# A copy on GpSimd ahead of each pair of row scatters, reading a tile of the Fourier step before

## The chip, the cores and the metric

One core of a Trainium2 chip runs the whole program. The metric is the device time of one execution in microseconds; the time before is the median of three executions. A profile was taken of one more execution.

## What is computed

Three parts follow one another. The Fourier part takes `x` (8 batches of 3072 rows of 256 numbers) through an FFT over the rows and one over the columns and keeps the real part. Each of the 24,576 rows that result is a token. A token whose score is not positive goes on unchanged; every other one is given to one of eight experts (argmax of eight logits), whose two matrices with a relu between them add to the row. At the end every row goes through a 256 to 2048 to 256 network with a rational activation.

```python
X = np.fft.fft(np.fft.fft(x, axis=1), axis=2).real        # 8 x 3072 x 256
do = X @ w_skip > 0;  e = argmax(X[do] @ w_gate)
X[do] += gate * (relu(X[do] @ w1[e]) @ w2[e])
h = X @ w_in
g = (a0 + a1*h + a2*h*h + a3*h**3) / (1 + |b0|*|h| + |b1|*h*h + 1e-6)
out = g @ w_out
```

## The kernel before

All matrix products run in pairs of 16-bit numbers (a high and a low half), so most tiles come twice, as `h` and `l`.

**Fourier part.** One loop (lines 609 to 641) makes 98 steps, `n` from 0 to 97; a batch takes 12 of them. In step `n`, in this order of issue:

- `s1_hi` (line 235, ScalarE) copies out the first-stage result of the chunk before;
- `s2` (lines 250 to 266): 12 matmuls with the first-stage tiles (line 260), then ScalarE writes the high half `o2h` (line 264) and VectorE the low half `o2l` (line 265). These tiles come from a pool of three buffers;
- `s3` for the tiles of two steps earlier (lines 308 to 310 on TensorE, `ev` on ScalarE at 314, three VectorE instructions at 315 to 317 that write finished rows and logits);
- `s1_lo` (lines 245 and 246);
- in two steps of three, as long as there is input (up to `n` = 83), the next first-stage chunk: loads of `x`, a split into halves (lines 192, 194 on ScalarE, 204 on VectorE; for three chunks of eight GpSimd makes the low half, line 202) and 24 matmuls (lines 225 to 227);
- one step of every open `route_steps` generator, and one of the generators that convert the weights (lines 386 to 433) and the coefficients (574).

`route_steps` (line 319) works on a finished batch. Seven of its steps find expert, gate and slot of every row with small VectorE instructions; the last of them writes the slot numbers `si` (line 358). Then come 24 row scatters (line 361): each is an indirect DMA, issued by GpSimd, that sends 128 rows of 258 numbers from SBUF to their slots in the DRAM table `xs`. In the loop `per` is 2: a pair of scatters is issued in each of 12 steps of the loop. For batch `bb` these are the steps from 12 bb + 20 on. What is written step by step is only the order on GpSimd's own queue, in which there is nothing but scatters, the low halves of line 202 and one memset; a scatter waits for its `si`, for its rows and for the scatter eight before it, and for nothing else of the step. The rows live in ten buffers (parts of the tiles `mw` and `third`); one is written again two steps after its second pair was issued (line 315 waits for those transfers). What remains of batch 6 when the loop ends (6 of its 12 pairs) is issued right behind the loop, and batch 7 is scattered in threes during the first tiles of the last part.

**Last part.** From line 1155 on, 48 tiles of 512 rows go through the rational network, with the expert work woven in. It takes most of the time. GpSimd runs the subtraction of line 1006 and the output scatters of line 1029 there. The first tile needs rows of batches 0 to 5 in `xs`, a conversion (line 885), a transpose by DMA (line 888) and the matmuls of line 897.

Of the kernel before, what the change touches and what calls it, by code (L numbers as in the profile page):

```python
# [8 lines left out]
F32 = mybir.dt.float32  # L9
F16 = mybir.dt.float16  # L10
# [7 lines left out]
B, SEQ, D = 8, 3072, 256  # L18
# [111 lines left out]
def program(tc, x, w_skip, w_gate, w1, w2, w_in, w_out, a, b, f1, cs, tw, tok, ut, small, lt8, slot, out):  # L130
    nc = tc.nc
    pe, act, dve, pool, sp = nc.tensor, nc.scalar, nc.vector, nc.gpsimd, nc.sync
    es = ExitStack()
    with es:
# [22 lines left out]
        cst = fa.enter_context(tc.tile_pool(name="cst", bufs=1))  # L157
# [16 lines left out]
        def new_u():  # L174
            return ps.tile([128, 2, 512], F32, tag="u", name="u")
# [56 lines left out]
        def s1_hi():  # L232
            if s1_open:
                u, oh, _, _ = s1_open[0]
                act.activation(oh, u[:, :, 0:384].rearrange("p h (q c) -> p h c q", q=4), AF.Copy)

        def s1_lo():

            if s1_open:
                u, oh, ol, c = s1_open.pop(0)  # L240
                if c < 7:
                    dve.tensor_tensor(out=ol, in0=u[:, :, 0:384].rearrange("p h (q c) -> p h c q", q=4), in1=oh, op=ALU.subtract)
                    return
                for h in range(2):
                    pe.matmul(u[:, h, 0:384].rearrange("p (q c) -> p c q", q=4), lhsT=nid[:], rhs=oh[:, h], start=False, stop=True, skip_group_check=True)  # L245
                act.activation(ol, u[:, :, 0:384].rearrange("p h (q c) -> p h c q", q=4), AF.Copy)

        o2 = {}

        def s2(bb, gp):  # L250
            u = ps.tile([128, 2, 512], F32, tag="u", name="u")
            for s in range(2):
                g = 2 * gp + s
                o = u[:, s, 0:CB]
                n = 0
                for h in range(2):
                    lh = o1[bb, "h"][:, h].rearrange("p c q -> p (c q)")[:, g * 128:g * 128 + 128]
                    ll = o1[bb, "l"][:, h].rearrange("p c q -> p (c q)")[:, g * 128:g * 128 + 128]
                    for st, mv in ((lh, 0), (lh, 1), (ll, 0)):
                        pe.matmul(o, lhsT=st, rhs=f2t[:, h, mv, :], start=(n == 0), stop=(n == 5))  # L260
                        n += 1
            th = o2p.tile([128, 2, CB], F16, tag="o2h", name="o2h")
            tl = o2p.tile([128, 2, CB], F16, tag="o2l", name="o2l")
            act.activation(th[:], u[:, :, 0:CB], AF.Copy, scale=2.0 ** -8)
            dve.scalar_tensor_tensor(out=tl[:], in0=u[:, :, 0:CB], scalar=2.0 ** -8, in1=th[:], op0=ALU.mult, op1=ALU.subtract)
            o2[bb, gp] = (th, tl)

        rows = {}
        lgs = {}
# [49 lines left out]
        def route_steps(bb, new_u, per=2):  # L319
            lg = lgs.pop(bb)  # L320
            rws = [rows.pop((bb, i)) for i in range(6)]
            lg8 = lg[:, :, 0:8]
            si = si_2[bb % 2]
            dve.tensor_reduce(out=mx, in_=lg8, op=ALU.max, axis=AX.X)
            dve.tensor_tensor(out=dd, in0=lg8, in1=mx.to_broadcast([128, NG, 8]), op=ALU.subtract)
            act.activation(ex, dd, AF.Exp, scale=16.0)
            yield
            dve.scalar_tensor_tensor(out=eq, in0=dd, scalar=0.0, in1=smt[:, None, 18:26].to_broadcast([128, NG, 8]), op0=ALU.is_equal, op1=ALU.mult)
            dve.tensor_reduce(out=mx, in_=eq, op=ALU.max, axis=AX.X)
            dve.tensor_scalar(out=cm, in0=lg[:, :, 8:9], scalar1=0.0, scalar2=None, op0=ALU.is_gt)  # L330
            dve.tensor_tensor(out=dd, in0=eq, in1=mx.to_broadcast([128, NG, 8]), op=ALU.is_equal)
            yield
            dve.tensor_tensor(out=oh[:, :, 0:8], in0=dd, in1=cm.to_broadcast([128, NG, 8]), op=ALU.mult)
            dve.tensor_scalar(out=oh[:, :, 8:9], in0=cm, scalar1=-1.0, scalar2=1.0, op0=ALU.mult, op1=ALU.add)
            dve.tensor_tensor(out=os_, in0=oh, in1=smt[:, None, 9:18].to_broadcast([128, NG, 9]), op=ALU.mult)
            yield
            yield
            u = new_u()
            for i in range(NG):
                pe.matmul(u[:, 0, 9 * (i + 1):225].rearrange("p (g c) -> p g c", c=9), lhsT=utt[:, 128:256],  # L340
                          rhs=os_[:, i:i + 1, :].to_broadcast([128, NG - i, 9]), start=(i == 0), stop=(i == NG - 1), skip_group_check=True)
            pe.matmul(u[:, 0, 0:216], lhsT=utt[:, 0:128], rhs=os_.rearrange("p g c -> p (g c)"), start=False, stop=True, skip_group_check=True)
            dve.tensor_reduce(out=sm, in_=ex, op=ALU.add, axis=AX.X)
            dve.tensor_scalar(out=sm, in0=sm, scalar1=1e-9, scalar2=None, op0=ALU.add)
            dve.reciprocal(out=sm, in_=sm)
            for i in range(6):
                dve.scalar_tensor_tensor(out=rws[i][:, :, D + 1:D + 2], in0=sm[:, 4 * i:4 * i + 4], scalar=2.0 ** -16, in1=cm[:, 4 * i:4 * i + 4], op0=ALU.mult, op1=ALU.mult)
                dve.tensor_scalar(out=rws[i][:, :, D:D + 1], in0=tokt[:, 4 * i:4 * i + 4, None], scalar1=float(bb * SEQ), scalar2=None, op0=ALU.add)
            yield
            dve.tensor_tensor(out=rk, in0=u[:, 0, 0:216].rearrange("p (g c) -> p g c", c=9), in1=carry[:, None, :].to_broadcast([128, NG, 9]), op=ALU.add)  # L350
            dve.tensor_tensor(out=carry[:], in0=carry[:], in1=u[:, 0, 216:225], op=ALU.add)
            if bb == B - 3:
                dve.tensor_scalar(out=carry[:, 8:9], in0=carry[:, 8:9], scalar1=float(SKIP0 + R0 * TILE), scalar2=None, op0=ALU.max)
                dve.tensor_scalar(out=carry[:, 0:1], in0=carry[:, 0:1], scalar1=float(R1 * HALF), scalar2=None, op0=ALU.max)
            yield
            dve.tensor_tensor(out=rk, in0=rk, in1=oh, op=ALU.mult)
            dve.tensor_reduce(out=sl[:, :, None], in_=rk, op=ALU.add, axis=AX.X)
            dve.tensor_copy(out=si, in_=sl)  # L358
            yield
            for g in range(NG):  # L360
                i = pool.indirect_dma_start(out=XS[:, :], out_offset=IndirectOffsetOnAxis(ap=si[:, g:g + 1], axis=0),  # L361
                                            in_=rws[g // 4][:, g % 4, :], in_offset=None, bounds_check=NROWS - 1, oob_is_err=False)
                if scat:
                    tc.declare_no_dep(i.ins, group="scat", reason="every slot is given once")
                tc.add_to_no_dep_group("scat", i.ins)
                if bb >= B - 2:
                    tc.add_to_no_dep_group("scat7", i.ins)
                scat.append(i.ins)
                if g % per == per - 1:
                    yield  # L370
# [229 lines left out]
        s1_hi()  # L600
        s1_lo()
        late = []
        prep = decode_steps()
        coeff = coefficients()
        n_dec = 8 * 6 + 4 * EARLY * 2
# [3 lines left out]
        for n in range(12 * B + LA):  # L609
            bb, gp = divmod(n, 12)  # L610
            s1_hi()
            if bb < B:
                s2(bb, gp)
            if n >= LA:
                s3(*divmod(n - LA, 12))
            s1_lo()
            if lo_next is not None:
                split_lo(lo_next)
                lo_next = None
            if c1 < 8 * B and gp % 3 != 2:  # L620
                load_x(c1 + 4)
                s1(c1)
                split_hi(c1 + 2)
                lo_next = c1 + 2
                c1 += 1
            if n >= LA and (n - LA) % 12 == 11 and n < 12 * B:
                late.append(route_steps((n - LA) // 12, new_u))
            for r in list(late):
                if next(r, 1) == 1:
                    late.remove(r)  # L630
            while decoded < min(n_dec, (n - 3) * n_dec // 84):
                next(prep, None)
                decoded += 1
            if n in (2, 4):
                load_tw(2 + n // 4)
            if n in (5, 7, 9, 11, 13):
                dummies((n - 5) // 2)
            if n >= 12:
                next(coeff, None)
                if n % 4 == 0:  # L640
                    next(coeff, None)
# [616 lines left out]
```

## Time and profile before

| | |
|---|---|
| median of three executions | 3161.35 us (3157.11 to 3165.08) |
| the profiled execution | 3152.81 us, span 3151.0 us |
| mean granted TensorE clock | 0.972 of full speed |
| busy share: TensorE, VectorE, ScalarE, GpSimd | 93%, 89%, 80%, 44% |
| chain that ended last | TensorE 75%, VectorE 13%, issue 5%, ScalarE 3%, DMA 3% |

The page gives busy times over the whole span and a strip of 40 slices of 79 us. The Fourier part is the first six slices or so; there TensorE and VectorE are busy by 60 to 90%, and behind it by over 90%. In the views, PE is TensorE (PEld its weight loads), ACT ScalarE, DVE VectorE, POOL GpSimd and SP the queue of SyncE. "issue" as the end of an idle time says that the engine waited for nothing that the profile shows. A wait put down to "remote" is one whose end the profile could not tie to an instruction.

### The profile page before, as it was taken

The page shows a single profiled execution, that of the slowest core. Times are in us where ns is not written, and L with a number is a line of the kernel's source. Part 1 is how long each engine was busy: PE and PEld are TensorE (multiplying, and loading weights), DVE is VectorE, ACT ScalarE, POOL GpSimd, SP SyncE. Part 2 cuts the span into 40 slices and gives each one's busy share as a digit, 9 for nine tenths or more (in the row PEclk, how much of TensorE's full clock was granted, in tenths as well). Part 3 has the DMA queues.
Part 4 walks back from the last instruction along what each step waited for, and adds up shares of the span by engine and source line. Part 5 has one row for each costly group of instructions (what it writes and reads, how often), then busy time and mean ns, then how long its engine had stood idle before and what let it go on. Part 6 is the DMA issues. An engine that isn't in the chain of part 4 may idle for free.

```text
span 3151.0 us, 56948 instructions
## 1 busy us (share of the span) xinstructions
PE 2944.4 (93%) x22994; PEld 2146.2 (68%) x22994; DVE 2816.8 (89%) x2969; ACT 2536.1 (80%) x2758; POOL 1391.3 (44%) x796
## 2 busy tenths in 40 slices
PE   8877864899999999999999999999999999999995
PEld 7666642577667777777777777777777777777764
DVE  6767644999999999999999999999999999999896
ACT  7666634698879889889889888888888888888884
POOL 0455534544334444444444444444444444444444
PEclk9989877999999999999999999999999999999998
DMA  8444443322312222213222311112112111211100
GB/s 237 148 145 133 157 161 114 92 84 68 108 41 68 55 88 85 67 45 93 82 58 65 86 43 34 40 57 67 35 41 81 45 31 41 84 38 28 31 18 14
DMA packets 230368, 236.85 MB, mean 75 GB/s; under 512 B 166995, under 2 KB 190932, under 8 KB 227156
## 3 DMA queue, kind: packets, MB, share of 16 engines
q1 hardware_dynamic: 209364, 174.23, 20.3%
q0 software_dynamic: 18432, 50.55, 4.6%
q10 hardware_dynamic: 2304, 8.39, 0.7%
q8 instruction: 181, 2.97, 0.4%
q14 instruction: 87, 0.71, 0.1%
HBM read 190.69 MB, written 77.05 MB: 85 GB/s over the span
## 4 chain that ended last, share of the span: by engine, by line
PE 75%; DVE 13%; issue 5%; ACT 3%; DMA 3%; another core or an unknown queue 1%; POOL 0%; SPq 0%; DVEq 0%; ACTq 0%; POOLq 0%
PE accz L907 26%; PE u L897 26%; PE acc L907 7%; PE e L897 7%; DVE gh L1000 4%; PE u L260 3%; DVE T L982 2%; DVE V L1005 2%; DMA out<-ob,ids 2%; PE u L245 1%; DVE gl L1012 1%; PE u L310 1%; DVE hl L915 1%; PE u L308 1%
## 5 line engine op out<-in xcount | busy, mean ns | idle before, releaser
L1006 POOL TENSOR_TENSOR V<-T,V 128x1024 f32<-128x1024 f32 x384 | 913.5, 2379 | 1369.8 <-DVE V L1005 1364.8
L897 PE MATMUL u<-turned,wi 128*128 128x512 f16 x4608 | 1065.3, 381 | 38.6 <-DMA turned<-rows 20.3
L907 PE MATMUL accz<-wo,gh 128*128 128x256 f16 x6144 | 1032.4, 273 | 5.9 <-ACT ob L1028 5.9
L907 PE MATMUL accz<-wo,gl 128*128 128x256 f16 x3072 | 839.9, 273 | 20.4 <-DVE gl L1012 18.0
L1000 DVE SCALAR_TENSOR_TENSOR gh<-T,co,Y 128x1024 f16<-128x1024 f32 x384 | 804.5, 2095 | 0.0
L897 PEld LDWEIGHTS <-wi 128*128 128x128 f16 x4608 | 452.7, 98 | 508.9 <-issue 50.7
L980 ACT ACTIVATE T<-u,co 128x1024 f32<-128x1024 f32 x384 | 462.8, 1205 | 331.3 <-PE u L897 202.5
L907 PEld LDWEIGHTS <-gh 128*128 128x128 f16 x6144 | 603.1, 98 | 159.3 <-issue 8.5
L982 DVE SCALAR_TENSOR_TENSOR T<-T,co,u 128x1024 f32<-128x1024 f32 x384 | 487.6, 1270 | 68.0 <-ACT Y L981 61.4
L1012 DVE SCALAR_TENSOR_TENSOR gl<-V,co,Y 128x1024 f16<-128x1024 f32 x384 | 489.0, 1274 | 28.8 <-POOL V L1006 28.8
L1005 DVE SCALAR_TENSOR_TENSOR V<-V,co,gh 128x1024 f32<-128x1024 f32 x384 | 490.3, 1277 | 0.0
L986 ACT ACTIVATE V<-Y,co 128x1024 f32<-128x1024 f32 x384 | 440.4, 1147 | 25.8 <-DVE gl L1012 25.6
L990 ACT ACTIVATE Y<-V,co 128x1024 f32<-128x1024 f32 x384 | 441.2, 1149 | 0.0
L981 ACT ACTIVATE Y<-u,co 128x1024 f32<-128x1024 f32 x384 | 426.3, 1110 | 0.0
L994 ACT ACTIVATE Y<-Y 128x1024 f32<-128x1024 f32 x384 | 404.3, 1053 | 0.0
L907 PEld LDWEIGHTS <-gl 128*128 128x128 f16 x3072 | 301.4, 98 | 60.1 <-DVE gl L1012 22.1
L897 PE MATMUL e<-turned,mw 128*128 128x256 f16 x2496 | 307.7, 273 | 8.1 <-DMA turned<-rows 8.1
L907 PE MATMUL acc<-mw,hh 128*128 128x256 f16 x1664 | 278.1, 273 | 0.0
L897 PEld LDWEIGHTS <-mw 128*128 128x128 f16 x2496 | 244.8, 98 | 37.3 <-issue 8.4
L1029 POOL DMA_INDIRECT out<-ob,ids x192 | 232.8, 1213 | 64.1 <-issue 46.4
L907 PE MATMUL acc<-mw,hl 128*128 128x256 f16 x832 | 226.8, 273 | 0.0
L361 POOL DMA_INDIRECT xs<-mw,rt x132 | 136.2, 1032 | 115.0 <-DVE rt L358 43.5
(201 smaller groups left out, 2942.5 us busy)
## 6 DMA issues: line engine op xcount, KB each, us to landing
mw<-wd SPq DMA_DIRECT2D x50, 2048.0 KB
xt<-in_x SPq DMA_DIRECT2D x64, 384.0 KB
xm<-xs SPq DMA_DIRECT2D x52, 258.0 KB
wf<-in_moe_w SPq DMA_DIRECT2D x48, 256.0 KB
wd<-ws SPq DMA_DIRECT2D x48, 256.0 KB
xt<-xs SPq DMA_DIRECT2D x22, 516.0 KB
wd<-ws ACTq DMA_DIRECT2D x16, 512.0 KB
wr<-in_moe_w_in SPq DMA_DIRECT2D x4, 1024.0 KB
```

What stands on the lines that cost most here:

```text
L897: pe.matmul(u[:, s, :], lhsT=sta, rhs=mv[:, :, k, :], start=(n == 0), stop=(n == 5))
L907: pe.matmul(acc[:, r, :], lhsT=sta[:, c], rhs=mv, start=(first and r % 2 == 0 and s == 0 and n == 0), stop=(last and s == nf - 1 and n == ...
L980: act.activation(d["T"], d["u"], AF.Square, scale=A[0], bias=A[1])
L981: act.activation(d["Y"], d["u"], AF.Abs, scale=A[4])
L982: dve.scalar_tensor_tensor(out=d["T"], in0=d["T"], scalar=A[2], in1=d["u"], op0=ALU.add, op1=ALU.mult)
L986: act.activation(d["V"], d["Y"], AF.Square, bias=A[5])
L990: act.activation(d["Y"], d["V"], AF.Ln, bias=A[6])
L994: act.activation(d["Y"], d["Y"], AF.Exp, scale=-1.0)
L1000: dve.scalar_tensor_tensor(out=h[:], in0=d["T"], scalar=A[a0], in1=d["Y"], op0=ALU.add, op1=ALU.mult)
L1005: dve.scalar_tensor_tensor(out=d["V"], in0=d["V"], scalar=A[c], in1=h[:], op0=ALU.add, op1=ALU.mult)
L1006: pool.tensor_tensor(out=d["V"], in0=d["T"], in1=d["V"], op=ALU.subtract)
L1012: dve.scalar_tensor_tensor(out=l[:], in0=d["V"], scalar=A[a0], in1=d["Y"], op0=ALU.add, op1=ALU.mult)
```

## The change

A tile `tick` is added. In each step, before `s2`, the name of the high-half tile that the step before made is kept; ahead of each pair of scatters of batches 0 to 6, GpSimd copies one 16-bit element per partition of that tile into `tick`. The copy has to wait for ScalarE's write of the tile, and the two scatters stand behind it on GpSimd's queue. In turn, ScalarE's write into the same buffer, three steps later, has to wait for the copy.

```diff
         o2 = {}
+        seen = [None]
+        tick = cst.tile([128, 1], F32, name="tick")
...
             o2[bb, gp] = (th, tl)
+            return th
...
             for g in range(NG):
+                if g % per == 0 and bb < B - 1:
+
+                    pool.tensor_copy(out=tick[:].bitcast(F16)[:, 0:1], in_=seen[0][:, 0, 0:1])
                 i = pool.indirect_dma_start(out=XS[:, :], out_offset=IndirectOffsetOnAxis(ap=si[:, g:g + 1], axis=0),
...
+        this = None
...
             s1_hi()
+            seen[0] = this
             if bb < B:
-                s2(bb, gp)
+                this = s2(bb, gp)
```

The orders of instructions on TensorE, VectorE and SyncE stay as they are. On GpSimd, in the steps 36 to 39 (batch 1, with two low halves of line 202 between scatters), it was:

```order
L361 DMA xs<-mw,rt 132096x258 [waits DMASW0_49]
L361 DMA xs<-mw,rt 132096x258 [waits DMASW1_49]
L202 TENSOR_TENSOR xl<-xt,xh 96x1024 [waits PE_49,Activation_49,Pool_49]
L361 DMA xs<-mw,rt 132096x258 [waits DMASW2_49]
L361 DMA xs<-mw,rt 132096x258 [waits DMASW3_49]
L202 TENSOR_TENSOR xl<-xt,xh 96x1024 [waits DVE_49,PE_49,Activation_49]
L361 DMA xs<-mw,rt 132096x258 [waits DMASW4_49]
L361 DMA xs<-mw,rt 132096x258 [waits DMASW5_49]
L361 DMA xs<-mw,rt 132096x258 [waits DMASW6_49]
L361 DMA xs<-mw,rt 132096x258 [waits DMASW7_49]
```

and is now (366 is the copy, 367 the scatter in the changed kernel's lines):

```order
L366 COPY tick<-o2h 128x1 [waits Activation_49,Pool_49]
L367 DMA xs<-mw,rt 132096x258 [waits DMASW0_49]
L367 DMA xs<-mw,rt 132096x258 [waits DMASW1_49]
L202 TENSOR_TENSOR xl<-xt,xh 96x1024 [waits PE_49,Activation_49]
L366 COPY tick<-o2h 128x1 [waits Pool_49]
L367 DMA xs<-mw,rt 132096x258 [waits DMASW2_49]
L367 DMA xs<-mw,rt 132096x258 [waits DMASW3_49]
L202 TENSOR_TENSOR xl<-xt,xh 96x1024 [waits DVE_49,PE_49,Activation_49]
L366 COPY tick<-o2h 128x1 [waits Pool_49]
L367 DMA xs<-mw,rt 132096x258 [waits DMASW4_49]
L367 DMA xs<-mw,rt 132096x258 [waits DMASW5_49]
L366 COPY tick<-o2h 128x1 [waits Activation_49,Pool_49]
```

84 copies are added (7 batches of 12 pairs). A copy behind a line 202 does not name ScalarE, because line 202 has waited for a later instruction of it already.

On ScalarE, the steps 83 and 84, where the input ends, read before:

```order
L235 ACTIVATE o1h<-u 128x192x4 [waits PE_49]
L264 ACTIVATE o2h<-u 128x552 [waits PE_49,Activation_49]
L314 ACTIVATE ev<-u 128x276 [waits PE_49,Activation_49]
L246 ACTIVATE o1l<-u 128x192x4 [waits PE_49]
L264 ACTIVATE o2h<-u 128x552 [waits DVE_49,PE_49]
```

and now:

```order
L235 ACTIVATE o1h<-u 128x192x4 [waits PE_49]
L266 ACTIVATE o2h<-u 128x552 [waits PE_49,Pool_49]
L317 ACTIVATE ev<-u 128x276 [waits PE_49,Activation_49]
L246 ACTIVATE o1l<-u 128x192x4 [waits PE_49]
L266 ACTIVATE o2h<-u 128x552 [waits DVE_49,PE_49,Pool_49]
```

The order is the same; what is new is that `o2h` waits for GpSimd.

## Rows read from the trace of the kernel before

**Rows 1.** The page's strip of 40 slices: granted TensorE clock in tenths.

```profile
PEclk9989877999999999999999999999999999999998
```

**Rows 2.** Stretches, all engines: busy us and instructions, granted clock, DMA share, GB/s.

```profile
31.53:98.46 66.93, 63.62 (x797) 53.11 (x795) 52.67 (x122) 56.84 (x83) 9.37 (x4) 0.99 0.67 200
102.27:448.41 346.14, 258.55 (x2759) 199.93 (x2757) 215.47 (x534) 198.03 (x296) 185.72 (x160) 0.87 0.46 144
448.41:490.84 42.43, 29.21 (x314) 24.53 (x312) 24.37 (x75) 13.05 (x25) 11.88 (x13) 0.91 0.47 178
490.84:521.20 30.36, 6.95 (x26) 3.09 (x26) 7.02 (x21) 3.04 (x6) 11.53 (x12) 0.51 0.46 160
```

**Rows 3.** The same stretches, line 264 (`o2h`, one per step) alone: ScalarE busy.

```profile
31.53:98.46 66.93, 11.91 (x19) 0.99 0.67 200
102.27:448.41 346.14, 40.13 (x64) 0.87 0.46 144
448.41:490.84 42.43, 6.89 (x11) 0.91 0.47 178
```

**Rows 4.** Timeline of GpSimd: first and last scatter of batches 5 and 6.

```profile
408.17 0.97 POOL L361 DMA_INDIRECT xs<-mw,rt  x1 [10.27 <-DVE rt L358]
...
437.84 0.98 POOL L361 DMA_INDIRECT xs<-third,rt  x1 [0.30 <-issue]
...
475.30 0.97 POOL L361 DMA_INDIRECT xs<-third,rt  x1 [36.48 <-DVE rt L358]
...
504.75 0.97 POOL L361 DMA_INDIRECT xs<-mw,rt  x1 [0.30 <-issue]
```

**Rows 5.** Timeline of TensorE towards the end of batch 5's scatters.

```profile
434.42 0.24 PE L226 MATMUL u<-f1t,xh 96*128 96x96 f16 x1 [1.16 <-issue]
435.82 0.24 PE L227 MATMUL u<-f1t,xl 96*128 96x96 f16 x1 [1.16 <-issue]
...
441.41 0.41 PE L260 MATMUL u<-f2t,o1h 128*128 128x276 f16 x1 [0.31 <-issue]
```

**Rows 6.** Waits of TensorE, 102 to 448 us: total us, times, longest.

```profile
PE u L260 <- issue: 11.4, 15, 1.9
PE u L227 <- issue: 10.2, 11, 1.9
PE u L225 <- issue: 8.9, 9, 1.7
PE u L245 <- issue: 8.8, 5, 3.5
```

**Rows 7.** Four stretches with scatters in twos and fours, line 264 alone.

```profile
129.05:141.70 12.65, 1.86 (x3) 1.00 0.57 171
189.04:204.37 15.33, 2.47 (x4) 1.00 0.35 105
248.31:261.06 12.75, 1.86 (x3) 1.00 0.60 177
372.21:389.50 17.29, 2.48 (x4) 1.00 0.69 222
```

**Rows 8.** The same four stretches, line 361 (scatters) alone: GpSimd busy.

```profile
129.05:141.70 12.65, 6.09 (x6) 1.00 0.57 171
189.04:204.37 15.33, 7.23 (x7) 1.00 0.35 105
248.31:261.06 12.75, 5.88 (x6) 1.00 0.60 177
372.21:389.50 17.29, 8.58 (x8) 1.00 0.69 222
```

**Rows 9.** Groups of GpSimd and VectorE, 102 to 448 us: busy us, mean ns, idle before.

```profile
L202 POOL TENSOR_TENSOR xl<-xt,xh 96x1024 f16<-96x1024 f32 x15 | 34.3, 2289 | 61.9 <-issue 55.3 <-ACT xh L194 6.5
L574 POOL MEMSET co<- 128x1 f32 x1 | 0.1, 126 | 0.0
L204 DVE SCALAR_TENSOR_TENSOR xl<-xt,xh 96x1024 f16<-96x1024 f32 x26 | 31.6, 1217 | 0.0
```

## The prediction

> **What bounds the kernel now.** I read the strip of the page first. The granted clock of TensorE is at nine tenths or above nearly everywhere, except in the slices up to 550 us, where it falls to seven [rows 1]. The change lies in that part, so the question is what the Fourier steps wait for. The next view is the busy time by stretch. In the first stretch, before any scatter, 19 steps take 66.93 us, 3.52 us each, at a clock of 0.99 [rows 2, 3]. From the first scatter to the 84th step, 64 steps take 346.14 us, 5.41 us each, at a clock of 0.87, and no engine is near full: TensorE is busy 258.55 us of it, VectorE 215, ScalarE 198, GpSimd 186. The DMA share is 0.46 there and was 0.67 in the quick stretch, so the transfers' bandwidth is not what slows it [rows 2].
>
> So something else stops the steps. The waits of TensorE show it: the four largest rows without a releaser add up to 39.3 us [rows 6], and they have no semaphore behind them. The timeline shows where they fall. While GpSimd sends 24 scatters without a break, one every 29.67 / 23 = 1.29 us [rows 4], TensorE, after about six quiet microseconds, gets one matmul of 0.24 us through every 1.4 us, with 1.16 us of "issue" before each [rows 5]. The last scatter starts at 437.84; at 441.41 the idle time before a matmul is down to 0.31 us and the steps run on. The counter-example is as plain: four stretches with 14 steps and 27 scatters, so nearly two per step, in which scatters come in twos and fours with other work or a pause between them, take 58.02 us, 4.14 us a step, at a clock of 1.00 [rows 7, 8]. So a scatter alone costs the steps little; an unbroken run of them stops TensorE, and the clock falls behind it. What couples the two no row tells. I take the link from these stretches and not from a mechanism.
>
> The steps stop because GpSimd runs ahead. Nothing ties a scatter to its step, so all 24 of batch 5 start at once when their slot numbers are there (the wait of 10.27 us ends on line 358), and those of batch 6 do the same [rows 4].
>
> **The change, part by part.** *The pairs are tied to the steps.* In steps 20 to 83 a pair can start only when the `o2h` of the step before is written. The unbroken runs in the stretch of 346.14 us become pairs with a pause. I price the steps by the stretches that look most like that: 4.14 us instead of 5.41. That is 64 x 4.14 = 265.0 us, a gain of 81.1 us. The bounds: the best that a row shows is the 3.52 us without any scatter, 225.3 us, a gain of 120.8; that stretch also has no coefficient or GpSimd work, so I take the nearer row. At the other end, if half of the stops stay, the step takes 4.78 us, 305.9 us, a gain of 40.
>
> *The copies.* 84 are added. The trace has no copy on GpSimd; the nearest row is the memset of one element per partition, 0.126 us [rows 9], the other bound is that a copy is held up as long as the longest VectorE instruction beside it, 1.217 us. I take 0.13. GpSimd then needs per step 2 x 1.29 for the pair, 0.13 for the copy and 34.3 / 64 = 0.54 for its share of the low halves: 3.25 us. The steps of 4.14 us cover it, with about 0.9 us to spare on average and some 1.4 us of pause in a step without a low half. If that cover goes, the steps cannot go below 3.25.
>
> *What is queued behind the new wait.* Behind a waiting copy stand its pair and then the low half of line 202, which the first-stage matmuls of a later chunk need. Those halves are made two chunks ahead, so a delay below a step is hidden. ScalarE gets the reverse wait: `o2h` three steps later needs the copy done. The copy runs in the step after its tile, so two steps, 8.3 us, of slack stand against the 3.25 us of work that GpSimd has per step: no cost. The third to wait is VectorE, whose rows of a step need the transfers of the pair one step before. That pair is released two steps before, 8.3 us, and takes 2.7 us to issue, so some 5.6 us are left for it to land: no cost either, but this is the term with the least slack after the pause.
>
> *The tail.* Steps 84 to 94 have no first stage and take 42.43 us, 3.86 each [rows 2, 3], with half of batch 6's run in them. In the new order the rest of batch 5's pairs falls here, 22 scatters where 13 were. The floor is GpSimd's 2.71 us per pair, 29.8 us, a gain of 12.6; as the pairs follow each other with hardly a pause, stops can come back here, and no change or even a loss is as possible. I take half of the floor's gain, 6.3 us.
>
> *The hand-over to the last part.* Twelve scatters ran on into the stretch of 30.36 us before the first tile of the last part [rows 2]; now it is one pair of the loop and six behind it, 14. Two more scatters are 2.6 us at most; I take nothing. The last part itself is untouched, and it starts earlier by what was gained.
>
> The sum is 81.1 + 6.3 = 87.4 us. On the profiled execution that is 3152.81 - 87.4 = 3065.4. The median of the three runs is 8.5 us above that execution, and the forecast is made on the median: **3074 us**.
>
> **A rule against it.** The low half on GpSimd takes 2.289 us on average [rows 9], and the rows don't say how much of that is waiting. The Trainium skill, page "SBUF — State Buffer", section "SBUF: two separate sides", says that VectorE and GpSimd share one pair of ports as an exclusive lock, and that a VectorE instruction with two SBUF inputs holds off a GpSimd instruction that reads SBUF. By that rule the copy, which reads SBUF, could wait for line 204; its price is the first rival's.
>
> **The rivals.**
>
> *The copy is held up, each time.* For it: line 204 takes 1.217 us and stands in the same steps [rows 9]. Against it: it runs 26 times in 64 steps, and GpSimd has 0.9 us to spare. Price: GpSimd needs 3.25 + 1.22 = 4.47 us per step, 64 x 4.47 = 286.1, a gain of 60, and nothing in the tail: 3101 us.
>
> *The pause is too short, and TensorE's stops come back: slower.* The pauses in the four good stretches are partly filled by a low half of over 2 us; the new one is 1.4 us, and no row shows that this is enough to end a run. If it isn't, a pair stops TensorE until 3.57 us after its second scatter [rows 4, 5], which is 0.13 + 1.29 + 3.57 = 5.0 us on top of the 4.14 of the step. It decides from one step in four on: (9.1 + 3 x 4.14) / 4 = 5.4, the step of now. With one step in three it is 5.8 us a step, 371 us, 25 us slower: 3186 us. Against it speaks that a stop delays the `o2h` that frees the next pair, so the run ends itself; before the change nothing ended it.
>
> *Nothing changes.* If the stops belonged to each scatter, wherever it stands, spreading them would not help: 39.3 us of idle over 144 scatters is 0.27 us each, before and after. 3161 us. Against it speak the 27 scatters at 1.00 of the clock and 4.14 us a step.
>
> *It goes further.* The clock stays up through the whole part and the steps fall to the 3.52 us of the start: 3161.35 - 120.8 - 12.6 = 3028 us. For it, that all of the slowing began with the first scatter.
>
> **How the numbers follow.** The forecast, a gain between 40 and 130 us, has 0.70; the held copy 0.10; the steps at their quickest 0.05; no change 0.07; the short pause 0.08. Faster by over 0.3% (9.5 us, about what a measurement of this kernel can tell from no change) is 0.85, within it 0.07, slower 0.08. The range goes from the quickest steps, 3030, to half of the stops staying, 3161.35 - 40 = 3121, rounded to 3122; it leaves out no change, the short pause and the ends of the two others, together about 0.2.
>
> **What would show it.** In the profile after, GpSimd's scatters stand in pairs with a copy of 0.13 us before each, the copies' idle time ends on `o2h`, and no run of more than a few scatters is left until the loop ends. TensorE's rows without a releaser fall from 39.3 us to below 10, the strip of its clock has no seven in the Fourier part but at its end, the 64 steps take about 265 us, and the last part starts some 87 us earlier and takes as long as before. It would be wrong if `o2h` waited for GpSimd (the copies or pairs too slow), if line 315 waited for transfers, if TensorE's stops stood between pairs, or if the steps stayed at 5.4 us with other waits in place of these.

## The result, and the profile after

The changed kernel takes 3084.09 us (median of four executions, 3074.85 to 3088.82), the kernel before beside it 3161.25 us (four, 3157.11 to 3165.08). The ratio is 0.9758, 95% interval 0.9739 to 0.9776: faster by 77 us. The forecast was 3074 us, its range 3030 to 3122.

That holds for the chip on which this comparison was made and, as the experiments show, not everywhere. On three others the kernel before takes 3045 to 3046 us, and on one of them, where it was tried, the changed kernel is 0.1% slower. What differs there is told below; it belongs to the result.

The stretches of the changed kernel, to be set against [rows 2] (steps 20 to 83, steps 84 to 94, and the beginning of the rest; busy us of PE, PEld, DVE, ACT, POOL, then granted clock, DMA share, GB/s):

```profile
101.41:389.72 288.31, 238.88 (x2759) 191.40 (x2757) 211.79 (x534) 196.31 (x296) 194.24 (x210) 0.95 0.55 171
389.72:429.51 39.79, 30.32 (x313) 25.52 (x312) 24.90 (x75) 13.15 (x25) 24.03 (x33) 0.93 0.56 198
429.51:460.00 30.49, 15.23 (x83) 7.41 (x83) 12.72 (x43) 11.74 (x15) 18.35 (x25) 0.74 0.57 186
```

The 64 steps take 288.31 us where they took 346.14, the clock there is 0.95 where it was 0.87, and the number of TensorE's instructions is the same. The waits of TensorE in this stretch, to be set against [rows 6] (total us, times, longest):

```profile
PE u L262 <- issue: 3.8, 7, 1.0
PE u L313 <- issue: 2.8, 6, 1.1
PE u L312 <- issue: 2.4, 4, 0.9
...
PE u L245 <- issue: 1.4, 3, 0.7
PE u L227 <- issue: 1.0, 2, 0.5
PE u L225 <- issue: 0.5, 1, 0.5
```

What were 11.4, 10.2 and 8.9 us in the three lines of second and first stage (260, 227, 225 before; 262, 227, 225 now) is 3.8, 1.0 and 0.5. With line 245 the four rows of [rows 6] fall from 39.3 to 6.7 us, below the 10 that the prediction gave as a sign. The groups of GpSimd in the same stretch (busy us, mean ns, idle before):

```profile
L202 POOL TENSOR_TENSOR xl<-xt,xh 96x1024 f16<-96x1024 f32 x15 | 34.2, 2277 | 19.5 <-ACT xh L194 16.0 <-ACT rt L580 3.4
L366 POOL COPY tick<-o2h 128x1 f16<-128x1 f16 x64 | 19.4, 303 | 21.7 <-ACT o2h L266 21.5 <-issue 0.2
```

The copies wait for `o2h`, as they should: 21.5 us in all. A copy takes 303 ns here (over all 84: 179 at least, 202 in the median, 1127 at most). In the timeline of GpSimd one sees pairs, and one sees what becomes of them behind a low half (line 202):

```profile
275.33 0.19 POOL L366 COPY tick<-o2h 128x1 f16<-128x1 f16 x1 [2.32 <-ACT o2h L266]
276.08 0.98 POOL L367 DMA_INDIRECT xs<-mw,rt  x1 [0.57 <-issue]
277.37 1.44 POOL L367 DMA_INDIRECT xs<-mw,rt  x1 [0.30 <-issue]
...
355.12 1.01 POOL L367 DMA_INDIRECT xs<-mw,rt  x1 [0.16 <-issue]
356.43 0.98 POOL L367 DMA_INDIRECT xs<-mw,rt  x1 [0.30 <-ACT ws L435]
357.40 0.20 POOL L366 COPY tick<-o2h 128x1 f16<-128x1 f16 x1
357.76 0.98 POOL L367 DMA_INDIRECT xs<-mw,rt  x1 [0.16 <-issue]
359.05 0.98 POOL L367 DMA_INDIRECT xs<-mw,rt  x1 [0.30 <-issue]
360.00 0.35 POOL L366 COPY tick<-o2h 128x1 f16<-128x1 f16 x1
360.50 0.99 POOL L367 DMA_INDIRECT xs<-mw,rt  x1 [0.15 <-issue]
361.79 0.97 POOL L367 DMA_INDIRECT xs<-mw,rt  x1 [0.30 <-issue]
```

At 275 us a copy waits 2.32 us, and its pair stands alone. At 355 us GpSimd is late: the tiles were written long ago, the copies wait for nothing, and three pairs make a run of six. Such runs keep some of TensorE's stops. A run of eight starts at 417.93 us, towards the end of the loop; TensorE beside it:

```profile
425.15 0.22 PE L312 MATMUL u<-o2l,twt 128*128 128x138 f16 x1 [1.16 <-issue]
...
426.58 0.22 PE L313 MATMUL u<-o2h,twt 128*128 128x138 f16 x1 [1.03 <-issue]
...
428.00 0.23 PE L313 MATMUL u<-o2h,twt 128*128 128x138 f16 x1 [1.08 <-issue]
```

The same picture as [rows 5], in few places instead of many.

### The profile page after: what moved, and what is told of

Read it like the earlier page. It is cut to its first block, busy times and chain, and to the rows that moved or that the text cites. A ratio compares the mean times of both kernels' runs of the same rounds, so it can differ in the third digit from the quotient of the medians.

```text
span 3082.0 us, 57108 instructions
## 1 busy us (share of the span) xinstructions
PE 2928.5 (95%) x22994; PEld 2137.2 (69%) x22994; DVE 2813.5 (91%) x2969; ACT 2533.9 (82%) x2758; POOL 1416.7 (46%) x880
## 4 chain that ended last, share of the span: by engine, by line
PE 69%; DVE 11%; issue 3%; DMA 2%; ACT 1%; POOL 1%; another core or an unknown queue 0%; DVEq 0%; POOLq 0%; ACTq 0%
PE accz L915 27%; PE u L905 26%; PE acc L915 8%; PE e L905 8%; DVE gh L1008 4%; DVE T L990 2%; DVE V L1013 2%; DMA out<-ob,ids 2%; DVE gl L1020 1%; DVE hl L923 1%; POOL out L1037 0%; DVE rows L894 0%; PE u L262 0%; POOL V L1014 0%
## 5 line engine op out<-in xcount | busy, mean ns | idle before, releaser
L905 PE MATMUL u<-turned,wi 128*128 128x512 f16 x4608 | 1067.3, 382 | 30.8 <-DVE T L990 17.3
L990 DVE SCALAR_TENSOR_TENSOR T<-T,co,u 128x1024 f32<-128x1024 f32 x384 | 487.7, 1270 | 75.0 <-ACT Y L989 57.8
L994 ACT ACTIVATE V<-Y,co 128x1024 f32<-128x1024 f32 x384 | 440.7, 1148 | 25.8 <-DVE gl L1020 25.6
L915 PEld LDWEIGHTS <-hh 128*128 128x128 f16 x1664 | 162.7, 98 | 19.0
```

The source lines that it names most:

```text
L905: pe.matmul(u[:, s, :], lhsT=sta, rhs=mv[:, :, k, :], start=(n == 0), stop=(n == 5))
L915: pe.matmul(acc[:, r, :], lhsT=sta[:, c], rhs=mv, start=(first and r % 2 == 0 and s == 0 and n == 0), stop=(last and s == nf - 1 and n == ...
L990: dve.scalar_tensor_tensor(out=d["T"], in0=d["T"], scalar=A[2], in1=d["u"], op0=ALU.add, op1=ALU.mult)
L994: act.activation(d["V"], d["Y"], AF.Square, bias=A[5])
```

## The experiments

Below, "idle" is the sum of TensorE's idle times of over 0.15 us that no releaser explains, matmuls and weight loads taken together, in steps 20 to 83; the hand-over reaches from the last `o2h` to the first `T` of the last part. All kernels but one are edits of the changed kernel. The first four ran on one chip, call it chip A, where the kernel before takes 3159.43 us (seven executions), so most likely the same or one like that of the comparison. The runs on A, B, C and D were made one after another, each chip once; what is called a difference between chips below could also be one between those times.

| kernel | chip | steps 20 to 83 | idle | steps 84 to 94 | hand-over | rest | time |
|---|---|---|---|---|---|---|---|
| before | | 346.1 | 55.4 | 42.4 | 30.3 | 2629.8 | 3161.25 |
| changed | | 288.3 | 13.2 | 39.8 | 16.8 | 2635.6 | 3084.09 |
| copies without a wait | A | 305.6 | 29.7 | 40.3 | 32.7 | 2629.4 | 3113.03 |
| pauses, no wait | A | 307.9 | 2.7 | 38.7 | 28.6 | 2646.3 | 3123.50 |
| fours | A | 317.2 | 21.8 | 45.3 | 17.0 | 2635.1 | 3117.04 |
| eights | A | 324.9 | 33.3 | 45.9 | 17.6 | 2633.5 | 3128.82 |
| batch 6 free | B | 259.9 | 0.0 | 33.5 | 19.6 | 2631.3 | 3048.26 |
| low halves on VectorE | B | 248.0 | 0.0 | 33.3 | 18.8 | 2632.9 | 3038.51 |
| last pairs apart | B | 260.6 | 0.0 | 32.6 | 20.0 | 2643.6 | 3063.34 |
| changed, again | C | 259.8 | 0.0 | 33.1 | 20.4 | 2629.6 | 3047.36 |
| low halves on VectorE, again | C | 248.0 | 0.0 | 32.6 | 20.0 | 2631.8 | 3037.01 |
| before, with added runs | C | 261.8 | 0.0 | 32.4 | 19.8 | 2630.9 | 3052.99 |

**Is it the wait, or the copy?** The copies stay, but read a constant, so that they wait for nothing.

```diff
-pool.tensor_copy(out=tick[:].bitcast(F16)[:, 0:1], in_=seen[0][:, 0, 0:1])
+pool.tensor_copy(out=tick[:].bitcast(F16)[:, 0:1], in_=nid[:, 0:1])
```

> The changed kernel, but each of the 84 copies reads a constant tile, so no pair waits for a Fourier step; the copies stay. Theory (the tie to the steps ends the unbroken runs): GpSimd runs ahead again, the runs come back nearly whole (a copy of 0.2 us and its overhead in each 2.6 us), the 64 steps take over 330 us and the time is near the kernel before, 3140 to 3161 us. Rival (the copies themselves break the runs): near the changed kernel, 3075 to 3095 us.

3113.03 us, ratio 0.9862 (0.9841 to 0.9883): between theory and rival. The copies still stand between the pairs and thin a run out a little, and that alone gives 40.5 of the 346.1 us of the steps back. The run of batch 6 still comes in one piece, and the hand-over stays at 32.7 us. The tie brings the rest: 17.3 us more in the steps and the whole of the hand-over.

**Is it the wait, or the pause?** Four memsets of 128x256, some 1.4 us, ahead of each pair in place of the copy; no wait.

```diff
-tick = cst.tile([128, 1], F32, name="tick")
+tick = cst.tile([128, 256], F32, name="tick")
...
-pool.tensor_copy(out=tick[:].bitcast(F16)[:, 0:1], in_=seen[0][:, 0, 0:1])
+for _ in range(4):
+    pool.memset(tick[:], 0.0)
```

> The changed kernel, but in place of each copy four memsets of 256 numbers per partition on GpSimd: a pause between pairs without any wait on a step. I estimate a pause of 1 to 1.6 us. Theory (a run stops TensorE because it is unbroken): the runs are cut into pairs with a pause, the time comes most of the way down, 3080 to 3115 us, with few waits without a releaser. Rival (the pairs must come at the pace of the steps; a pause changes nothing): 3140 us or more.

3123.50 us, ratio 0.9891 (0.9873 to 0.9908), in neither range. TensorE's idle falls to 2.7 us, the lowest on this chip, so a pause ends the stops with no tie at all. But GpSimd now has some 4 us of work per step besides its low halves (a pair and its pause), falls behind, and VectorE waits for the transfers of the rows that it writes next:

```profile
DVE mw L318 <- DMA xs<-mw,rt: 39.2, 17, 6.3
DVE third L318 <- DMA xs<-third,rt: 22.2, 10, 5.7
```

In the changed kernel that wait is 1.8 us. The tie costs GpSimd only a copy, and is the better pause here.

**How long may a run be?** One copy ahead of four scatters in every second step, then ahead of eight in every fourth.

```diff
-if g % per == 0 and bb < B - 1:
+if g % 4 == 0 and bb < B - 1:
...
+elif g % 4 == 4 - 1:
+    for _ in range(4 // 2):
+        yield
```

> One size changed: in batches 0 to 6 four scatters behind one copy in every second step, in place of two in every step; the rate stays. Theory (TensorE's stops begin some 6 us after the start of an unbroken run): a run of four is over after 5.1 us, so the time is that of the changed kernel within 15 us, 3070 to 3100 us. Rival (each bunching costs in proportion): half of the way from runs of two to runs of eight, 3100 to 3130 us.

> The same with eight scatters behind one copy in every fourth step. A run of eight takes 10.2 us, so by the theory TensorE stops in the last third of each run, some 2.5 us of waits without a releaser per run, 21 runs: 3110 to 3150 us. If the length of a run does not matter and only the rate over a batch does: 3075 to 3095 us as with pairs.

Fours take 3117.04 us (ratio 0.9862, 0.9839 to 0.9885), the rival's range; eights 3128.82 us (0.9911, 0.9888 to 0.9934), the theory's. Pairs, fours, eights and untied runs give 13.2, 21.8, 33.3 and 55.4 us of idle and 288.3, 317.2, 324.9 and 346.1 us for the steps: the longer the run, the longer the stops. "Untied" is a mixture here: between GpSimd's low halves the scatters of five batches come in runs of 2, 4, 8 and 10, and only those of batch 5 in one run of 24, beside which 19.6 of the 55.4 us lie. I had missed that two fours meet: in nine places a late four and the next one make a run of eight, and mostly 5 to 11 us after its first scatter the stops begin; in the run of eights it is mostly 5 to 10 us. The steps grow by more than the idle. TensorE's busy time in them (the first number behind the comma) is 238.88 us with pairs, at a clock of 0.95, and with fours and eights:

```profile
101.29:418.48 317.19, 254.92 (x2760) 200.35 (x2757) 214.66 (x533) 198.90 (x296) 182.43 (x178) 0.90 0.50 153
101.43:426.34 324.91, 260.16 (x2759) 203.21 (x2757) 210.18 (x533) 198.38 (x297) 177.61 (x162) 0.88 0.48 149
```

**What of a scatter stops TensorE?** Three runs of twelve transfers into scratch tables were added where nothing else scatters: wide rows, narrow rows, and rows whose indices are all out of bounds.

```diff
...
+if n in (2, 8, 14):
+    burst(("wide", "narrow", "none")[(n - 2) // 6])
```

> Added work: in the steps before the first real scatter, three unbroken runs of 12 indirect transfers each into scratch tables that nothing reads: in step 2 rows of 258 numbers, in step 8 rows of 32 numbers, in step 14 rows of 258 whose indices are all out of bounds, so that nothing is to be stored. Each run lasts some 15.5 us. In the changed kernel these steps have no issue idle on TensorE. Theory A (the bytes that the transfers move stop TensorE): only the first run gives stops, from some 6 us after its start, 5 us or more of issue idle in all; the second and third give under 1 us. Theory B (the making of the transfers by GpSimd stops it, whatever they move): all three runs give about the same idle, 5 us or more each. Theory C (the number of row transfers in the queues): the first two alike, the third under 1 us. The whole is slower than the changed kernel by no more than 30 us.

One execution took 3063.06 us, and none of the three runs stopped TensorE. It was not the added runs that were harmless: this set of runs came to another chip, B, on which the kernel before takes 3046.35 us (16 executions, 3041.80 to 3053.76), and there TensorE's steps show no stop in any kernel. The 17 us that steps 0 to 19 lose come from GpSimd's low halves, queued behind the added runs (TensorE waits 12.8 us for them). On the cause this run says nothing.

The other three kernels of this set ran on chip B too, so they answer less than they were made for.

```diff
-if g % per == 0 and bb < B - 1:
+if g % per == 0 and bb < B - 2:
```

> The copy is left out for batch 6 alone, so its 24 scatters start as soon as their slots are there. Theory (the hand-over gained because the run of batch 6 was broken up): steps 20 to 83 stay within 3 us of the changed kernel's 288.3, the hand-over goes back from 16.8 to about 30 us and the last part's start loses nothing, so some 6 to 14 us slower than the changed kernel, 3090 to 3098 us. Rival (the hand-over's gain comes from elsewhere, the earlier steps): hand-over stays below 20 us, 3080 to 3088 us.

3048.26 us, ratio to the kernel before 1.0005 (0.9994 to 1.0016). The run of 24 of batch 6 is back, and the hand-over is 19.6 us against 20.4 with the tie on chip C. Where TensorE does not stop, there is nothing to gain here; what the tie of batch 6 is worth on a chip with stops was not tried.

```diff
 def by_pool(c):
-    return c >= 12 and c % 8 in POOLC
+    return False
```

> All low halves of x are made by VectorE, none by GpSimd; copies and pairs as in the changed kernel. Theory (what is left of the stops comes from steps in which GpSimd catches up behind a low half and sends four or more scatters in a row): the issue idle of TensorE in steps 20 to 83 falls from 13.2 to below 5 us, and runs longer than 4 scatters become rare. VectorE gets 15 x 1.2 = 18 us more work in 64 steps, so the steps take between 4.3 and 4.7 us: 3070 to 3097 us. Rival (the stops that are left belong to pairs as such): issue idle stays at 10 us or more, 3090 to 3110 us.

3038.51 us, ratio 0.9973 (0.9959 to 0.9986). The steps fall to 248.0 us, 3.88 each, though VectorE has 15 low halves more. There are no stops here to end, so this gain is another one. The theory's other half did not come true: runs of six scatters and more did not become rare (ten with gaps of at most 0.65 us, nine in the changed kernel of the comparison). The edit also does more than it seems: ScalarE no longer scales those chunks ahead of the low half (line 192, 15 instructions, 15.7 us in these steps on chip C). The same edit on chip C, with the columns of the rows after:

```profile
101.16:349.18 248.02, 223.30 (x2760) 185.14 (x2758) 214.53 (x549) 184.43 (x282) 168.62 (x194) 0.99 0.61 190
```

ScalarE is busy 184.43 us where the changed kernel has 198.05, and VectorE 214.53 where it has 217.27: its 15 low halves cost 18.3 us, but its lines 328, 338 and 580 fall from 25.8 to 8.5 us. Which of these makes the steps quicker no run separates. The changed kernel on chip C (below) has one more row that bears on it, the copies of the same steps:

```profile
L366 POOL COPY tick<-o2h 128x1 f16<-128x1 f16 x64 | 22.1, 345 | 3.3 <-ACT o2h L266 3.3
```

Its copies wait for `o2h` 3.3 us in all, where it was 21.5 with stops: GpSimd, not ScalarE, is late in these quicker steps. Of its work there the low halves are 34.6 us, the copies 22.1 and the scatters 140.5.

```diff
-seen = [None]
-tick = cst.tile([128, 1], F32, name="tick")
+seen = [None, False]
+tick = cst.tile([128, 256], F32, name="tick")
...
+for _ in range(4 if seen[1] else 0):
+    pool.memset(tick[:], 0.0)
...
+seen[1] = True
 for r in late:
```

> Four memsets (some 1.3 us of GpSimd) ahead of each of the six pairs of batch 6 that are left when the loop ends; all else as in the changed kernel. Theory (the 16 scatters there run unbroken and stop TensorE in the hand-over and the first tiles): the 9.6 us of issue idle in the hand-over and the 3.4 us behind it fall to below 5 together, hand-over 11 to 14 us, and the whole is 3 to 9 us quicker than the changed kernel, 3075 to 3081 us. Rival (the hand-over waits for the scatters themselves to land): it grows by the 8 us of the pauses, 3088 to 3093 us.

3063.34 us, ratio 1.0053 (1.0033 to 1.0072), 15 us behind the kernel with batch 6 free on the same chip. The hand-over is 20.0 us and does not grow. The 9.6 us of idle that the theory set out to remove were not stops but one wait, for the first transposed rows (shown further down). The loss is in the last part. The first weights of the experts are loaded into `mw`, where the late rows still lie, and TensorE waits for that load, first here, then with batch 6 free:

```profile
PEld L908 <- DMA mw<-wd: 20.1, 1, 20.1
```

```profile
PEld L905 <- DMA mw<-wd: 7.9, 1, 7.9
```

**The change and the kernel before, on another chip.** The changed kernel as it is; its variant without low halves on GpSimd; and the kernel before, with the three added runs ahead of step 20 (its low halves start later, so that none stands behind them).

> The changed kernel as it is, beside the kernel before, on the chip that this set of runs gets. Theory (the gain is the end of TensorE's stops, and whether a run of scatters stops TensorE differs from chip to chip): where the kernel before takes about 3160 us, the ratio is 0.974 to 0.978 again; where it takes about 3046 us, the changed kernel has no issue idle in steps 20 to 83, steps of about 260 us, and a ratio of 0.998 to 1.003. Rival (the tie gains by itself, by the order in which GpSimd works): the ratio is below 0.99 on either chip.

> The changed kernel with all low halves of x on VectorE, a second time. Theory (two separate gains: no steps in which GpSimd catches up, and, on a chip with stops, fewer of them): 7 to 14 us quicker than the changed kernel on a chip without stops (3032 to 3042 us); on a chip with stops 0 to 25 us quicker (3060 to 3085 us), its issue idle in steps 20 to 83 below 10 us. Rival (VectorE becomes the bound on a chip with stops): no quicker than the changed kernel there.

> The kernel before (pairs not tied), with three added unbroken runs of 12 indirect transfers into scratch tables in the steps before the first real scatter: rows of 258 numbers in step 2, rows of 32 numbers in step 8, all indices out of bounds in step 14. GpSimd's low halves begin only with chunk 26, so that none stands behind an added run. Its later steps show the kernel before on this chip. On a chip with stops: theory A (the bytes stop TensorE): only the first run gives issue idle, 3 us or more from about 6 us after its start, the others under 0.5 us; theory B (the making of the transfers): all three give 3 us or more; theory C (the number of transfers that are carried out): the first two, not the third. On a chip without stops: none gives any, and the untied runs of 24 in steps 20 to 83 give under 2 us in place of the 55.4 us seen before.

On this chip, C, the kernel before takes 3045.25 us (21 executions), the changed one 3047.36: ratio 1.0012 (1.0003 to 1.0021), so 2.1 us slower. The rival, a gain from the tie itself, falls. Steps 20 to 83 and 84 to 94, first of the changed kernel, then of the untied one:

```profile
102.00:361.76 259.76, 226.97 (x2760) 186.21 (x2758) 217.27 (x533) 198.05 (x297) 195.81 (x209) 0.98 0.58 182
361.76:394.89 33.13, 27.62 (x293) 23.21 (x291) 23.96 (x72) 13.04 (x26) 20.50 (x30) 0.95 0.67 250
```

```profile
106.32:368.13 261.81, 228.79 (x2759) 188.07 (x2757) 218.42 (x534) 197.99 (x296) 174.63 (x146) 0.97 0.58 180
368.13:400.55 32.42, 27.21 (x293) 22.92 (x291) 24.36 (x75) 13.04 (x25) 17.52 (x18) 0.95 0.73 284
```

The untied kernel needs 261.81 us for the steps that took it 346.14 [rows 2], with hardly a change in its order (four low halves, all ahead of step 20, are on VectorE). And it has its long runs there, too. GpSimd in the middle of a run of twenty, and TensorE at that time, ten microseconds and more into the run:

```profile
369.44 0.97 POOL L364 DMA_INDIRECT xs<-mw,rt  x1 [0.31 <-issue]
370.72 0.97 POOL L364 DMA_INDIRECT xs<-mw,rt  x1 [0.30 <-issue]
372.00 0.97 POOL L364 DMA_INDIRECT xs<-mw,rt  x1 [0.30 <-issue]
```

```profile
370.14 0.22 PE L312 MATMUL u<-o2l,twt 128*128 128x138 f16 x1
370.20 0.22 PE L313 MATMUL u<-o2h,twt 128*128 128x138 f16 x1
370.26 0.23 PE L311 MATMUL u<-o2h,twt 128*128 128x138 f16 x1
...
371.04 0.28 PE L262 MATMUL u<-f2t,o1l 128*128 128x276 f16 x1
371.16 0.40 PE L262 MATMUL u<-f2t,o1h 128*128 128x276 f16 x2
```

GpSimd issues one scatter every 1.28 us, as in [rows 4]; TensorE starts a matmul every 0.06 to 0.12 us, where [rows 5] had 1.16 us of "issue" before each. The runs are the same; whether they stop TensorE differs from chip to chip, or with something else that is the same for a whole set of runs. The added runs did not stop it either, so theories A to C stay open.

**The quickest version on the chips without stops.** Without low halves on GpSimd the changed kernel takes 3037.01 us on chip C, ratio to the kernel before 0.9977 (0.9968 to 0.9986), 10.4 us quicker than the changed kernel beside it. The last run put the added runs into this version:

> The changed kernel with all low halves on VectorE, and the three added runs of 12 transfers in steps 2, 8 and 14 (rows of 258, rows of 32, all out of bounds). On a chip where the kernel before takes about 3045 us: no issue idle in steps 0 to 83, the added runs cost 3 to 8 us ahead of step 20, steps 20 to 83 take 246 to 250 us, the whole 3037 to 3047 us. On a chip where it takes about 3160 us: steps 20 to 83 between 260 and 290 us with less than 13 us of issue idle; of the added runs all three stop TensorE by 3 us or more (the making of the transfers), or the first two alone (transfers that are carried out), or the first alone (their bytes).

It came to a fourth chip, D, where the kernel before takes 3046.45 us (15 executions), and gave 3040.55 us, ratio 0.9979 (0.9970 to 0.9988), with steps of 247.4 us and no idle. So on the three chips on which TensorE does not stop this version is 0.2 to 0.3% quicker than the kernel before (on D with the added runs in it); the changed kernel ran beside it on C alone. On a chip with stops it was not run.

## Why the prediction was right, and where it was off

**The reading of the bound held.** The stops belong to unbroken runs [rows 4 to 6]: thinning a run, pausing it or shortening it each cut the idle, in order of the length of the run. The idle is not the whole loss: TensorE is busy 258.55 us in these steps before [rows 2] and 228.79 us, for the same matmuls, in the untied kernel on chip C. In the trace's record of the granted clock 88.7 us of the steps lie at the lower of its two levels before and 30.0 us in the changed kernel, on chip C 17.1 (untied) and 10.2 (changed); the time at the upper level is 257.4, 258.4, 244.7 and 249.5 us. The stops do not need the low clock: 31.3 of the 55.4 us of idle lie at the upper level. The rival "nothing changes" assumed that the stops belong to each scatter; on the chips with stops it falls, since all kernels send the same number. On chip C hardly anything changes after all, and for a reason that I had not among the rivals: there is nothing there to end. The trace of before could not show this; it comes from one chip.

**The step of 4.14 us was mis-sized.** "I price the steps by the stretches that look most like that: 4.14 us instead of 5.41", a gain of 81.1 us, was the largest term; it measured 288.31 / 64 = 4.50 us and 57.8 us. Chip C shows what the 4.14 us was: there the changed kernel's steps take 259.76 / 64 = 4.06 us. The four stretches [rows 7, 8] were steps without any stop, so they gave the floor; I took it for what pairs would reach. Pairs end two thirds of the loss (57.8 of 346.1 - 259.8 = 86.3 us). The other third is left because pairs join into runs of four to ten whenever GpSimd is late, behind a low half or late slot numbers, as the timeline at 355 us shows. The same 14 steps take 4.10 us each in the changed kernel too, and 4.19 on chip C: there was nothing in them to gain. With stops the sixth and eleventh step of a batch still take 6.3 and 6.5 us on average, those at the stretches' places 2.9 to 5.8. The rival "the pause is too short" was right that no row showed the pause to be enough; it did not decide. After the stops at 425 us the next copy waits 2.28 us for `o2h`, so a stop holds back the pair behind it, as the prediction had it.

**The copies** were put at 0.13 us, from a memset; they take 0.30 us in the steps. With two scatters of 1.09 us (141.7 us for 130) and the 0.30 us between instructions GpSimd still fits into a step of 4.50 us, so the 0.17 us per step above the estimate were hidden. What is not quite hidden is the reverse wait, put at no cost: `o2h` waits for a copy 3.5 us in all (twice) in the run of the comparison, and 10.9 us (five times, 1.7 us of it in steps 20 to 83) on chip C. Whether that is the 2.1 us that the change loses there is not shown.

**The held copy** happened now and then and not each time: 1127 ns at most, 202 in the median. 15 of the 84 copies take over 0.35 us, and each of them stands beside a VectorE instruction with two SBUF inputs. The longest ends with it:

```profile
245.82 1.23 DVE L402 SCALAR_TENSOR_TENSOR wf<-wr,wf 128x1024 int32<-128x1024 int32 x1
245.96 1.13 POOL L366 COPY tick<-o2h 128x1 f16<-128x1 f16 x1
```

VectorE is held up too, the other way round. Line 328, with two SBUF inputs, takes 0.36 us in the median; once it stands beside GpSimd's low half and takes 2.82 us, until that has ended. In the 14 traces of this case the two overlap 20 times, and each time it takes 1.04 to 2.92 us; in the other 92 cases it takes 0.36:

```profile
288.41 2.82 DVE L328 TENSOR_TENSOR rt<-rt 128x192 f32<-128x192 f32 x1
```

```profile
288.85 2.15 POOL L202 TENSOR_TENSOR xl<-xt,xh 96x1024 f16<-96x1024 f32 x1
```

The Trainium skill, page "SBUF — State Buffer", section "SBUF: two separate sides", says that the two engines share a pair of ports under an exclusive lock; the trace agrees, in that the two stood in each other's way here (the copy of 1.13 us, the line 328 of 2.82), but rarely, and as a bound of this change it does not appear.

**The tail** was put at a gain of 6.3 us and gave 42.43 - 39.79 = 2.6: at 418 us the slots of batch 6 come late and eight scatters follow each other, with the stops shown at 425 us. **The hand-over** was put at no change ("I take nothing") and gained 30.3 - 16.8 = 13.5 us. I had counted scatters there and not what their run does to the last steps of the loop. Before, ScalarE waits 16.25 us for one `ev`, until 3 us after the run's last scatter has started [rows 4], and the conversion that the first tile needs is queued behind it on ScalarE, with the transpose after that. First before, then now:

```profile
507.77 0.40 ACT L314 ACTIVATE ev<-u 128x276 f32<-128x276 f32 x1 [16.25 <-remote]
516.42 4.75 PE L897 MATMUL u<-turned,wi 128*128 128x512 f16 x12 [20.34 <-DMA turned<-rows]
```

```profile
432.52 0.40 ACT L317 ACTIVATE ev<-u 128x276 f32<-128x276 f32 x1 [1.75 <-issue]
442.07 4.25 PE L905 MATMUL u<-turned,wi 128*128 128x512 f16 x12 [9.64 <-DMA turned<-rows]
```

The last `ev` starts 18.7 us behind the last `o2h` before, 3.0 now; with copies without a wait, where the run is back, it is 21.0, and in the untied kernel on chip C, beside a run as long, 2.4. How the run holds it back is not shown: the matmuls that it waits for are recorded by 496 us. TensorE's own idle is no measure of stops here, since nearly all of it (20.3 of 22.5 us, then 9.6) is the one wait for the transposed rows. **The last part** was to take as long as before and lost 2635.6 - 2629.8 = 5.8 us: 4.2 ahead of its second `T`, beside the last of 16 scatters that run from 431 to 452 us, and 1.6 between 874 and 921 us, where no scatter of the loop is left (chip C has this second part as well, 1.5 us).

The sum on the two profiled executions: 57.8 + 2.6 + 13.5 - 5.8, and 0.9 us ahead of step 20, make 69.0 us, the difference of the spans (3151.0 and 3082.0). The medians differ by 77 us. Against the sum of 87.4 us that is 18.4 too little on the profiled executions: the gain of the steps was put 23.3 us too high, that of the tail 3.7 and the last part 5.8, and the hand-over, put at nothing, made up for 13.5 of it, with the 0.9. That it did was luck. The time came out only 10 us above the forecast because the profiled execution of the kernel before was 8.5 us quicker than the median on which the forecast stands. The slack given to VectorE's rows was there: line 318 waited 1.8 us for transfers.

## What to carry to other kernels

Where an engine stops without a releaser, look what another engine does unbroken at that time, and break it up; the cheapest break tried here is a wait on something that the loop makes anyway, since it costs a copy of 0.3 us and no fixed pause, but it breaks nothing where the engine that waits is already late. A stretch of a trace that is free of a disturbance gives the floor that an edit can reach, not what it will reach. And a loss that shows on one chip need not be there in the runs on the next: measure before and after on several, or a change that gains 2.4% on one and loses 0.1% on another looks like only one of the two.

## What was not expected of the hardware

- The same program differs by 3.7% between the runs on one chip and those on three others: 3159.43 us on A, and 3046.35, 3045.25 and 3046.45 us on B, C and D. Each chip was met once, so chip and time are not told apart. By the stretches of the table (the kernel before, and the one with added runs on chip C), steps 20 to 83 make 84.3 us of it, steps 84 to 94 10.0 and the hand-over 10.5; the rest, from the first `T` on, is the same to 1.1 us.
- On a chip with stops an unbroken run of indirect transfers from GpSimd lets single matmuls through only every 1.4 us at its worst ([rows 5], and the timeline at 425 us), mostly from 5 to 10 us after its start. Neither the scatters' own pace (1.28 us each on either kind of chip) nor the DMA share (in the changed kernel 0.55 with stops, 0.58 without) tells the chips apart. What couples the two engines stays open.
